# Rotary attention and two expert layers on one core: the opening cut into pieces, and pair 1's rotations dealt out between row maxima

## The chip, the cores and the metric

One of the eight cores of a Trainium2 chip runs the whole program. The metric is the device time of one execution in microseconds (us), lower is better.

## The reference, cut to what matters

```python
# q, k, v: 4 batches x 8 heads x 576 positions x 64, float32
q_rot, k_rot = rotate(q), rotate(k)        # x1*cos - x2*sin, x1*sin + x2*cos
scores = q_rot @ k_rot^T / 8
attn = exp(scores - rowmax(scores)); attn /= rowsum(attn) + 1e-9
x = attn @ v                               # -> 2304 tokens x 512
# layer 1: the best of 8 experts for each token, relu(x @ w1[e]) @ w2[e] * gate
# layer 2: relu(x @ w_in)^2 @ w_out        # 2304 x 512 -> 2048 -> 512
```

## The kernel before, in words

**Stages.** Attention comes first, then routing and the experts, then the dense layer. Attention works on 16 pairs P of heads. The change touches only the first two pairs.

**A pair.** `load(P)` brings the tile `qk`: 128 partitions, the values and their swapped halves (w), keys and queries (n = 0, 1), 640 columns. `rotate` is three passes: multiply by the cosine, multiply by the sine, add. `high` copies the sum into a tile `XH` in the fast float format on ScalarE; `low` puts the remainder into `XL`. For pairs from 1 on `stack_up` copies pieces of both into the tiles kZ, qZ and QH by DMA; for pair 0 `direct_high` and `direct_low` write them with ScalarE and VectorE. Then come nine row tiles s = 0 to 8. For each of them there are three steps, written here as S(P,s), the products on TensorE (`scores`), M(P,s), the row maximum on VectorE (`smax`), and X(P,s), the exponential on ScalarE (`sexp`). The scores have two PSUM buffers, so a third S waits for the X two before it. `turn` transposes exponentials on TensorE, `turned` copies them out on VectorE or ScalarE, `values`, `project` and `finish` do the rest.

**Who rotates.** Pairs 0 and 1 are rotated on VectorE, in `prepare`. From pair 2 on GpSimd does it, in three steps (`rope`, lines 394 to 396), and `low` without an engine argument is on GpSimd as well, for pair 1 too.

**The order.** Each engine carries out its instructions in the order in which the program issues them. `prepare()` is issued first; everything after it is put on a list with a due time, `OFF[...] + 15.954 * P`, and issued in the order of these times. The due times only sort; they are not waited for. The ones that matter here, in that unit:

```python
rope of pair 2 (GpSimd)          20.629, 23.559, 26.489
S(1,2) (TensorE)                 31.625
high(2) (ScalarE)                32.143
S(1,8) (TensorE)                 33.025
X(1,2) (ScalarE)                 33.433
low(2) (GpSimd)                  33.583
S(1,4) (TensorE)                 34.689
```

So on ScalarE `high(2)` stands ahead of X(1,2), and on GpSimd `low(1)`, issued by `prepare`, stands ahead of the three rope steps of pair 2. `prepare` also puts 14 products of 512 columns on TensorE ahead of pair 0's scores (line 169), and `scores` of pair 0 begins with two products whose result is overwritten (line 266).

Of the kernel before, what the change touches and what calls it, by code (L numbers as in the profile page):

```python
# [10 lines left out]
F32 = mybir.dt.float32  # L11
# [48 lines left out]
def shape_constants():  # L60
# [27 lines left out]
    for b in range(B):  # L88
        for c in range(4):
# [21 lines left out]
           un=[32.589, 32.153, 35.217, 38.036, 36.617, 23.748, 28.906, 37.6, 35.653, 34.253, 33.817],  # L111
           out=[33.418, 34.148, 36.917, 39.025, 37.411, 29.788, 32.958, 38.405, 36.294, 35.538, 34.643],
           av=[41.194, 44.969], x=[46.747, 47.789], pj=54.426, fin=58.03)
ON_DVE = [(0, 0), (0, 3), "LQ", "CR", (1, 0), (1, 1), (1, 3)]


def attention(tc, rope, ident, qk, v, w_gate, xd, on_batch, later, ahead):
# [24 lines left out]
    def ppt(name, shape=(128, 512)):  # L142
        return psa.tile(list(shape), F32, name=name, tag="pp", bufs=4)

    def prepare():
        nc.scalar.dma_start(out=TB[:, :, 0], in_=rope)
        load(0)
        load(1)
        for t in Xs:
            nc.gpsimd.memset(t[:, 576:640], 0.0)  # L150
        for t in SS:
            nc.gpsimd.memset(t[:, :, 1:2], 1e-9)
        for two in QH:
            for j in range(2):
                nc.gpsimd.memset(two[j][64 - 64 * j:128 - 64 * j].bitcast(F32), 0.0)
        nc.gpsimd.memset(R, 0.0)
        for r in range(2):
            d = slice(64 * r, 64 * r + 64)
            nc.gpsimd.tensor_copy(R[d, :, r, 0:64], ident[d, d].unsqueeze(1).broadcast_to([64, 4, 64]))
        for o, lo, hi in ((0, 64, 640), (576, 0, 64)):  # L160
            nc.scalar.activation(TB[:, :, 1, o:o + hi - lo], TB[:, :, 0, lo:hi], AF.Copy, scale=0.125)
        for j in range(2):
            Z = T["qZ", j] = zp.tile([128, 640], F32R, name="qZ", tag="qZ", bufs=4)
            nc.gpsimd.memset(Z[64 - 64 * j:128 - 64 * j, 0:512].bitcast(F32), 0.0)
        rotate(0, 0, nc.vector)
        high(0, 0)
        w = ppt("warm")
        for i in range(14):
            nc.tensor.matmul(w, T["hi", 0][:, 0, 0:128], T["hi", 0][:, 0, 0:512], start=True, stop=True)
        rotate(0, 1, nc.vector)  # L170
        direct_high(0)
        low(0, 0, nc.vector)
        direct_low(0, nc.vector)
        load(2)
        rotate(1, None, nc.vector)
        high(1)
        low(1)
        load_v(0)
        stack_up(1)

    def direct_high(P):


        x, h = T["qk", P], T["hi", P]
        for j in range(2):
            r = slice(64 * j, 64 * j + 64)
            nc.scalar.activation(QH[P][j][r], x[r, 0, 1, 0:512], AF.Copy)
        nc.scalar.activation(h[:, 1, 512:640], x[:, 0, 1, 512:640], AF.Copy)

    def direct_low(P, eng):  # L190
        x = T["qk", P]
        for j in range(2):
            r = slice(64 * j, 64 * j + 64)
            minus(eng, T["qZ", 2 * P + j][r, 0:512], x[r, 0, 1, 0:512], QH[P][j][r].bitcast(F32))
        minus(eng, T["lo", P][:, 1, 512:640], x[:, 0, 1, 512:640], T["hi", P][:, 1, 512:640].bitcast(F32))

    def gate_weights():
        for r in range(2):
# [3 lines left out]
    def load(P):  # L202
        t = T["qk", P] = ldp.tile([128, 2, 2, 640], F32, name="qk", tag="qk", bufs=2)
        src = qk[P].rearrange("p (w n c) -> p w n c", w=2, n=2)
        if P == 0:
            for n in range(2):
                nc.sync.dma_start(out=t[:, :, n], in_=src[:, :, n])
        else:
            nc.sync.dma_start(out=t, in_=src)

# [1 line left out]
        V = T["V", P] = wp.tile([128, 2, 5, 64], F32, name="V", tag="V", bufs=2)  # L212
        nc.sync.dma_start(out=V, in_=v[P].rearrange("p (h c d) -> p h c d", h=2, c=5))

    def rotate(P, n, eng, step=None):
        x, a = T["qk", P], slice(0, 2) if n is None else slice(n, n + 1)
        for i, (f, o, y) in enumerate(((times, 0, TB[:, 0, a]), (times, 1, TB[:, 1, a]), (plus, 0, x[:, 1, a]))):
            if step in (None, i):
                f(eng, x[:, o, a], x[:, o, a], y)

    def high(P, n=None):

        if ("hi", P) not in T:
            T["hi", P] = zp.tile([128, 2, 640], F32R, name="XH", tag="XH", bufs=2)
        a = slice(0, 2) if n is None else slice(n, n + 1)
        nc.scalar.activation(T["hi", P][:, a], T["qk", P][:, 0, a], AF.Copy)

    def low(P, n=None, eng=None):
        if ("lo", P) not in T:
            T["lo", P] = zp.tile([128, 2, 640], F32R, name="XL", tag="XL", bufs=2)  # L230
        a = slice(0, 2) if n is None else slice(n, n + 1)
        args = T["lo", P][:, a], T["qk", P][:, 0, a], T["hi", P][:, a].bitcast(F32)
        if eng is None:
            nc.gpsimd.tensor_sub(*args)
        else:
            minus(eng, *args)

    def stack_up(P, n=None):

        h, l = T["hi", P].bitcast(F32), T["lo", P].bitcast(F32)  # L240
        for j in range(2):
            r = slice(64 * j, 64 * j + 64)
            q = nc.scalar if P == 0 and j == 1 else nc.sync
            if n != 1:
                Z = T["kZ", 2 * P + j] = zp.tile([128, 640], F32R, name="kZ", tag="kZ", bufs=4)
                for i in range(2):
                    q.dma_start(out=Z[64 * i:64 * i + 64].bitcast(F32), in_=h[r, 0])
            if n != 0:
                Z = T["qZ", 2 * P + j] = zp.tile([128, 640], F32R, name="qZ", tag="qZ", bufs=4)
                q.dma_start(out=Z[0:64].bitcast(F32), in_=h[r, 1])  # L250
                q.dma_start(out=QH[P % 2][j][r].bitcast(F32), in_=h[r, 1, 0:512])
                q.dma_start(out=Z[64:128].bitcast(F32), in_=l[r, 1])

    def scores(P, s):

        t = T["S", P, s] = ps.tile([128, 2, 512], F32, name="ps", tag="ps", bufs=2)
        if s < 8:
            j, c = divmod(s, 4)
            todo, qs, qh = [j], slice(c * 128, c * 128 + 128), QH[P % 2][j]
            qh = qh[:, qs]  # L260
        else:
            todo, qs, qh = [0, 1], slice(512, 640), T["hi", P][:, 1, 512:640]
        k0 = 0 if s in (4, 5, 6, 7) else 64
        if P == 0:
            for u in range(2):
                nc.tensor.matmul(t[:, u, 0:288], QH[0][0][:, 0:128], T["hi", 0][:, 0, 0:288], start=True, stop=True)
            H, L = T["hi", P], T["lo", P]
            ql = L[:, 1, 512:640] if s == 8 else T["qZ", 2 * P + j][:, qs]
            for i, (q1, k1) in enumerate(((qh, H), (ql, H), (qh, L))):
                for u in range(2):  # L270
                    nc.tensor.matmul(t[:, u, 0:288], q1, k1[:, 0, k0 + 288 * u:k0 + 288 * u + 288], start=i == 0, stop=i == 2)
            return
        for i, j in enumerate(todo):
            Q1, K1 = T["qZ", 2 * P + j], T["kZ", 2 * P + j]
            for u in range(2):
                nc.tensor.matmul(t[:, u, 0:288], Q1[:, qs], K1[:, k0 + 288 * u:k0 + 288 * u + 288], start=i == 0, stop=False)  # L276
        for u in range(2):
            nc.tensor.matmul(t[:, u, 0:288], qh, T["lo", P][:, 0, k0 + 288 * u:k0 + 288 * u + 288], start=False, stop=True)  # L278
# [103 lines left out]
            at(t, lambda: route(P, t))  # L382

    prepare()
    at(24.0, gate_weights)
    for P in range(NPAIR):
        def on(o, f, *args):
            at(OFF["pair"] * P + o, lambda: f(*args))

        if P > 2:  # L390
            on(OFF["load"], load, P)
        if P > 0:
            on(OFF["v"] + (1.8 if P == NPAIR - 1 else 0), load_v, P)
        if P > 1:
            for i in range(3):
                on(OFF["rope"] + 2.93 * i, rotate, P, None, nc.gpsimd, i)
            on(OFF["hi"], high, P)
            on(OFF["lo"], low, P)
            on(OFF["z"], stack_up, P)
        for s in range(9):  # L400
            on(OFF["S"][s], scores, P, s)
            on(OFF["max"][s], smax, P, s)
            on(OFF["exp"][s], sexp, P, s)
        for un, o, o2 in zip(UNITS, OFF["un"], OFF["out"]):
            on(o, turn, P, un)
            on(o2, turned, P, un)
        for u in range(2):
            on(OFF["av"][u], values, P, u)
            on(OFF["x"][u], gathered, P, u)
        on(OFF["pj"], project, P)  # L410
        on(OFF["fin"], finish, P)
        if P % 4 == 3 and P + 1 < NPAIR:
            on(OFF["fin"] + .02, route, P)
# [10 lines left out]
def minus(v, out, a, b):  # L424
    v.tensor_tensor(out=out, in0=a, in1=b, op=ALU.subtract)
# [836 lines left out]
```

## Time and profile before

| | |
|---|---|
| median of 3 runs | 981.23 us (980.25 to 981.56) |
| profiled execution: its own time, its span | 979.74 us, 977.8 us |
| TensorE busy over the span | 953.0 us (97%) |
| VectorE, ScalarE, GpSimd busy | 530.7, 421.4, 322.0 us |
| attention, from the start to the last `project` | about 297 us |

The page shares the span out in 40 slices of 24.4 us. TensorE is at 4 tenths in the first slice and at 9 in all others but the last, at 7. In the trace the nine X of pair 0 start at 19.84, 20.56, 22.87, 23.94, 25.92, 27.41, 28.96, 30.46 and 32.00 us; the one that starts at 33.90 is X(1,2). All times below are us from the start of the span. The timeline merges neighbours of one kind: "x2" is two instructions, and the duration is from the start of the first to the end of the last.

### The profile page before, as it was taken

How to read it: one execution, taken by the hardware profiler on the slowest of the kernel's cores; microseconds unless marked ns; L12 is line 12 of the kernel's file. 1: busy time of each engine (PE TensorE's matmuls, PEld its weight loads, DVE VectorE, ACT ScalarE, POOL GpSimd, SP SyncE). 2: the span in 40 equal slices, each digit the busy share in tenths (PEclk: the TensorE clock that was granted, in tenths of full speed). 3: DMA queues.
4: the chain of work that ended last, by engine and by line, in shares of the span. 5: the costliest groups of instructions: out<-in, count | busy, mean ns of one | idle time of the engine just before them, and what ended most of it. 6: DMA issues, size and time to landing. Idle time of an engine off the chain costs nothing. (4 is left out here: it accounts for less than half of the span.)

```text
span 977.8 us, 15396 instructions
## 1 busy us (share of the span) xinstructions
PE 953.0 (97%) x5519; PEld 817.1 (84%) x5519; DVE 530.7 (54%) x935; ACT 421.4 (43%) x834; POOL 322.0 (33%) x259
## 2 busy tenths in 40 slices
PE   4999999999999999999999999999999999999997
PEld 3787878788787888888888789999999999999996
DVE  5677877777867255683785479423323323223221
ACT  3666657575642233343464377422322322222221
POOL 4786887887485111241353300010000100100101
PEclk9999999999999999999999999999999999999999
DMA  6876777866642833364586433100100201000000
GB/s 229 247 198 193 233 210 189 254 179 165 184 130 89 306 107 127 116 206 153 186 284 219 145 99 120 33 33 1 44 22 1 65 1 33 33 1 1 33 1 33
DMA packets 45135, 119.81 MB, mean 123 GB/s; under 512 B 8176, under 2 KB 8176, under 8 KB 42608
## 3 DMA queue, kind: packets, MB, share of 16 engines
q1 hardware_dynamic: 39808, 101.58, 33.7%
q0 software_dynamic: 4960, 16.43, 4.9%
q8 instruction: 45, 0.74, 0.3%
q10 hardware_dynamic: 272, 0.66, 0.2%
q14 instruction: 50, 0.41, 0.1%
HBM read 79.93 MB, written 15.11 MB: 97 GB/s over the span
## 5 line engine op out<-in xcount | busy, mean ns | idle before, releaser
L1088 PE MATMUL o<-Wo,gs 128*128 128x512 f32 x864 | 215.0, 393 | 0.4 <-ACT gs L1077 0.4
L1067 PE MATMUL h<-xs,Wi 128*128 128x384 f32 x1008 | 189.6, 336 | 0.0
L1088 PEld LDWEIGHTS o<-Wo,gs 128*128 128x128 f32 x864 | 159.8, 188 | 29.3 <-ACT gs L1077 0.8
L1067 PEld LDWEIGHTS h<-xs,Wi 128*128 128x128 f32 x1008 | 178.2, 188 | 6.6
L1076 DVE SCALAR_TENSOR_TENSOR g<-h,r 128x384 f32<-128x384 f32 x80 | 44.6, 558 | 190.7 <-ACT r L1072 190.7
L293 ACT ACTIVATE e<-ps,mx 128x576 f32<-128x576 f32 x144 | 106.2, 740 | 83.1 <-DVE mx L286 82.9
L1103 POOL DMA_INDIRECT out_dram<-os,at x18 | 17.9, 992 | 369.9 <-DVE os L1098 310.7
L286 DVE TENSOR_REDUCE mx<-ps 128x1 f32<-128x576 f32 x144 | 105.9, 753 | 57.2 <-PE ps L278 50.4
L1072 ACT ACTIVATE r<-h 128x384 f32<-128x384 f32 x96 | 47.1, 490 | 204.7 <-PE h L1067 204.7
L890 PE MATMUL p_y<-W,hh 128*128 128x512 f32 x504 | 122.9, 399 | 0.8 <-ACTq L902 0.8
L861 PE MATMUL p_h<-W,xs 128*128 128x512 f32 x480 | 114.9, 394 | 0.0
L890 PEld LDWEIGHTS p_y<-W,hh 128*128 128x128 f32 x504 | 93.1, 188 | 22.2 <-ACTq L902 1.1
L861 PEld LDWEIGHTS p_h<-W,xs 128*128 128x128 f32 x480 | 88.5, 188 | 18.4 <-DVEq L902 0.7
L311 PE MATMUL pp<-ident,e 128*128 128x128 f32 x640 | 85.5, 273 | 1.3 <-DVE eT L327 1.0
L1078 DVE TENSOR_TENSOR gs<-g,gs 128x384 fp32r<-128x384 f32 x96 | 53.5, 558 | 56.0 <-ACT gs L1077 56.0
L433 POOL TENSOR_TENSOR qk<-qk,TB 128x1280 f32<-128x1280 f32 x28 | 81.4, 2923 | 0.0
L311 PEld LDWEIGHTS pp<-ident,e 128*128 128x128 f32 x640 | 74.5, 141 | 2.6 <-DVE eT L327 1.6
L1077 ACT ACTIVATE gs<-g 128x384 fp32r<-128x384 f32 x96 | 50.4, 525 | 50.5 <-DVE g L1076 50.0
L276 PE MATMUL ps<-kZ,qZ 128*128 128x288 f32 x300 | 71.5, 328 | 0.3
L338 PE MATMUL av<-eT,V 128*64 128x288 f32 x512 | 69.1, 412 | 0.0
L327 DVE COPY eT<-pp 128x512 f32<-128x512 f32 x96 | 64.3, 684 | 4.6 <-PE pp L311 2.7
L895 POOL DMA_INDIRECT yd<-yo,idx x21 | 21.2, 1012 | 126.5 <-DVE yo L894 94.6
(237 smaller groups left out, 1208.7 us busy)
## 6 DMA issues: line engine op xcount, KB each, us to landing
qk<-in_qk_dram SPq DMA_DIRECT2D x15, 1280.0 KB, 6.5
raw<-in_moe_w_dram SPq DMA_DIRECT2D x30, 512.0 KB, 5.1
kZ<-XH SPq DMA_DIRECT2D x60, 160.0 KB, 2.8
rawa<-in_moe_w_dram SPq DMA_DIRECT2D x18, 512.0 KB, 3.5
w<-in_moe_w_in_dram SPq DMA_DIRECT2D x8, 1024.0 KB, 5.4
w<-in_moe_w_out_dram SPq DMA_DIRECT2D x8, 1024.0 KB, 5.0
V<-in_v_dram SPq DMA_DIRECT2D x16, 320.0 KB, 2.9
qZ<-XH SPq DMA_DIRECT2D x30, 160.0 KB, 2.9
```

What stands on the lines that cost most here:

```text
L276: nc.tensor.matmul(t[:, u, 0:288], Q1[:, qs], K1[:, k0 + 288 * u:k0 + 288 * u + 288], start=i == 0, stop=False)
L286: nc.vector.tensor_reduce(small("mx", P, 9)[:, s:s + 1], T["S", P, s][:, :, 0:288], axis=AX.XY, op=ALU.max, negate=True)
L293: nc.scalar.activation(ed.rearrange("p (u n) -> p u n", u=2), T["S", P, s][:, :, 0:288], AF.Exp, bias=T["mx", P][:, s:s + 1], accum_out=SS ...
L311: nc.tensor.transpose(t[:, c * 128:c * 128 + 128], src, ident)
L327: nc.vector.tensor_copy(o, i)
L338: nc.tensor.matmul(t[64 * j:64 * j + 64], V[:, j, kc], eT[:, j, kc, cs] if kc < 4 else eL[:, cs], start=kc == 0, stop=kc == 4)
L433: v.tensor_tensor(out=out, in0=a, in1=b, op=ALU.mult)
L861: nc.tensor.matmul(t[u], s[:, a, k], W1[:, b, k, 512 * u:512 * u + 512], start=n == 0, stop=n == 11)
L890: nc.tensor.matmul(t, s[:, a, k], W2[:, b, k], start=n == 0, stop=n == 23)
L1067: nc.tensor.matmul(t, W[:, a, k, fs], s[:, c, k], start=n == 0, stop=n == 11)
L1078: nc.vector.tensor_sub(gs[:, 1], g, gs[:, 0].bitcast(F32))
L1088: nc.tensor.matmul(self.T["o", b][c], gs[:, a, 128 * c:128 * c + 128], W[:, w], start=(f == 0 and n == 0), stop=(f == 15 and n == 2))
```

## The change

`prepare` loads the rope tables and pair 0 in column pieces, rotates and splits them piece by piece (keys in two halves of 320, queries as A = 0 to 256 and Z = 256 to 640), and issues 30 products of the identity with itself in place of the 14 large ones. What followed in `prepare` moves into a list, `opening()`, whose due times 0.0, 0.1, ... put it before all else. Pair 1 is no longer rotated in one go of three passes over 1280 columns; it is six passes over 640 (keys, then queries), and they alternate on VectorE with pair 0's maxima. `high(1)`, `low(1)` and `stack_up(1)` follow in halves. The two idle products of pair 0's scores move behind the real ones. Four of pair 0's transposes (FIRST) get due times of 29.5 to 30.1 and come ahead of S(1,2). The due times of all other work stay.

```diff
+FIRST = [(0, 1), (0, 0), (1, 3), (1, 2)]
+    HALF, A, Z = (slice(0, 320), slice(320, 640)), slice(0, 256), slice(256, 640)
     def prepare():
-        nc.scalar.dma_start(out=TB[:, :, 0], in_=rope)
+        for h in HALF:
+            nc.scalar.dma_start(out=TB[:, :, 0, h], in_=rope[:, :, h])
...
-        for o, lo, hi in ((0, 64, 640), (576, 0, 64)):
+        for o, lo, hi in ((0, 64, 320), (256, 320, 640), (576, 0, 64)):
             nc.scalar.activation(TB[:, :, 1, o:o + hi - lo], TB[:, :, 0, lo:hi], AF.Copy, scale=0.125)
-        rotate(0, 0, nc.vector)
-        high(0, 0)
-        w = ppt("warm")
-        for i in range(14):
-            nc.tensor.matmul(w, T["hi", 0][:, 0, 0:128], T["hi", 0][:, 0, 0:512], start=True, stop=True)
-        rotate(0, 1, nc.vector)
-        direct_high(0)
+        T["warm"] = ppt("warm")
+        keep_warm(nc, ident, T["warm"][:, 0:128], 30)
+        for h in HALF:
+            rotate(0, 0, nc.vector, cols=h)
+            high(0, 0, h)
+        rotate(0, 1, nc.vector, cols=A)
+        direct_high(0, A)
         low(0, 0, nc.vector)
-        direct_low(0, nc.vector)
-        load(2)
-        rotate(1, None, nc.vector)
-        high(1)
-        low(1)
-        load_v(0)
-        stack_up(1)
+        direct_low(0, nc.vector, A)
+    def opening():
+        two = lambda s: (lambda: scores(0, s), lambda: smax(0, s), lambda: sexp(0, s))
+        S, M, X = [dict(zip(range(9), [two(s)[n] for s in range(9)])) for n in range(3)]
+        step = lambda n, i: lambda: rotate(1, n, nc.vector, i)
+        return [S[0], S[1], lambda: rotate(0, 1, nc.vector, cols=Z), lambda: direct_high(0, Z), M[0], X[0], M[1], X[1],
+                lambda: direct_low(0, nc.vector, Z), lambda: load(2), S[4], S[5], step(0, 0), M[4], X[4], step(0, 1), M[5], X[5],
+                step(0, 2), S[8], S[2], M[8], X[8], lambda: high(1, 0), lambda: stack_up(1, 0),
+                step(1, 0), M[2], X[2], step(1, 1), S[3], S[6], M[3], X[3], step(1, 2), lambda: high(1, 1), M[6], X[6],
+                lambda: low(1, 1), lambda: low(1, 0), lambda: stack_up(1, 1), lambda: load_v(0), S[7], M[7], X[7]]
...
     def load(P):
-        if P == 0:
-            for n in range(2):
-                nc.sync.dma_start(out=t[:, :, n], in_=src[:, :, n])
+        if P < 2:
+            for n, c in ([(0, h) for h in HALF] + [(1, A), (1, Z)] if P == 0 else [(n, slice(0, 640)) for n in range(2)]):
+                nc.sync.dma_start(out=t[:, :, n, c], in_=src[:, :, n, c])
...
     prepare()
+    for n, f in enumerate(opening()):
+        at(.1 * n, f)
...
-        for s in range(9):
+        for s in range(9) if P else ():
...
+            if P == 0 and un in FIRST:
+                o, o2 = [t + .2 * FIRST.index(un) for t in (29.5, 29.6)]
```

`keep_warm` is `for i in range(n): nc.tensor.matmul(out, ident, ident, start=True, stop=True)`, in float32. `stack_up` now issues, for each head of a pair, first the kZ copies (n != 1) and then qZ from XH, QH, and qZ from XL (n != 0), all on SP.

## Rows read from the trace of the kernel before

**Rows 1.** Stretches of attention: sum and mean of the five from 34.77 to 240.
```profile
sum 205.23, PE 205.03 PEld 168.20 DVE 154.12 ACT 136.05 POOL 161.40; mean PE 41.01 PEld 33.64 DVE 30.82 ACT 27.21 POOL 32.28
```
**Rows 2.** Timeline, pair 1 to pair 2: start, duration, engine, line, tile<-sources, count [idle before].
```profile
18.66 1.27 ACT L226 ACTIVATE XH<-qk 128x1280 fp32r<-128x1280 f32 x1 [5.14 <-DVE qk L429]
20.08 2.93 POOL L234 TENSOR_TENSOR XL<-qk,XH 128x1280 fp32r<-128x1280 f32 x1 [13.65 <-ACT XH L226]
22.96 5.80 POOL L433 TENSOR_TENSOR qk<-qk,TB 128x1280 f32<-128x1280 f32 x2
28.85 2.93 POOL L429 TENSOR_TENSOR qk<-qk 128x1280 f32<-128x1280 f32 x1
32.73 1.26 ACT L226 ACTIVATE XH<-qk 128x1280 fp32r<-128x1280 f32 x1
33.90 0.73 ACT L293 ACTIVATE e<-ps,mx 128x576 f32<-128x576 f32 x1
34.77 0.53 PE L276 MATMUL ps<-kZ,qZ 128*128 128x288 f32 x2
```
**Rows 3.** Timeline of VectorE in the opening.
```profile
7.12 1.56 DVE L433 TENSOR_TENSOR qk<-qk,TB 128x640 f32<-128x640 f32 x2 [6.13 <-DMA qk<-in_qk_dram]
9.46 1.55 DVE L433 TENSOR_TENSOR qk<-qk,TB 128x640 f32<-128x640 f32 x2
11.79 0.82 DVE L425 TENSOR_TENSOR XL<-qk,XH 128x640 fp32r<-128x640 f32 x1
12.57 1.41 DVE L425 TENSOR_TENSOR qZ<-qk,QH 64x512 fp32r<-64x512 f32 x2
14.22 2.89 DVE L433 TENSOR_TENSOR qk<-qk,TB 128x1280 f32<-128x1280 f32 x2
18.55 1.41 DVE L286 TENSOR_REDUCE mx<-ps 128x1 f32<-128x576 f32 x2
```
**Rows 4.** DMA of the first loads: KB each and us to landing.
```profile
TB<-in_rope_dram ACTq DMA_DIRECT2D x1, 640.0 KB, 4.6
qk<-in_qk_dram SPq DMA_DIRECT2D x1, 640.0 KB, 6.3
```
**Rows 5.** DMA queue from 5 to 6, then 9 to 10: packets, MB, share.
```profile
q1 hardware_dynamic: 155, 0.40, 102.2%
...
q1 hardware_dynamic: 40, 0.41, 97.0%
```
**Rows 6.** Timeline, when the identity stands ready on GpSimd.
```profile
1.16 0.28 POOL masks.py:199 TENSOR_SCALAR_AFFINE_SELECT ident<-ident 128x128 f32<-128x128 f32 x1
```
**Rows 7.** Timeline of TensorE: the 14 products, two of the scores, a `project`.
```profile
10.37 6.32 PE L169 MATMUL warm<-XH 128*128 128x512 f32 x14 [10.37 <-ACT XH L226]
...
16.79 0.42 PE L271 MATMUL ps<-XH,QH 128*128 128x288 f32 x2
...
54.13 1.39 PE L349 MATMUL pj<-R,X 128*128 128x144 f32 x10
```
**Rows 8.** Timeline, one turn of pair 0's ring of scores.
```profile
26.61 0.76 DVE L286 TENSOR_REDUCE mx<-ps 128x1 f32<-128x576 f32 x1 [0.73 <-PE ps L271]
...
27.41 0.74 ACT L293 ACTIVATE e<-ps,mx 128x576 f32<-128x576 f32 x1 [0.66 <-DVE mx L286]
...
28.29 0.54 PE L266 MATMUL ps<-XH,QH 128*128 128x288 f32 x2 [0.17 <-ACT e L293]
...
29.67 0.76 DVE L286 TENSOR_REDUCE mx<-ps 128x1 f32<-128x576 f32 x1 [0.75 <-PE ps L271]
```
**Rows 9.** The copies of `stack_up`: an issue on SP, and landing times of qZ.
```profile
26.11 0.60 SPq L252 DMA_DIRECT2D qZ<-XL  x1
...
DMA to landing us min/median/max: 2.6/2.9/3.2
```
**Rows 10.** The end of the span: TensorE's last products, and a stretch after them.
```profile
966.55 5.27 PE L1088 MATMUL o<-Wo,gs 128*128 128x512 f32 x21 [0.40 <-ACT gs L1077]
...
975.50:976.00 0.50, 0.00 (x0) 0.00 (x0) 0.00 (x0) 0.00 (x0) 0.00 (x0) 0.68 0.01 0
```

More of the change, by code (lines that the diff above doesn't have):

```diff
@@ L155, in prepare @@
                 nc.gpsimd.memset(two[j][64 - 64 * j:128 - 64 * j].bitcast(F32), 0.0)
+        for j in range(2):
+            q = T["qZ", j] = zp.tile([128, 640], F32R, name="qZ", tag="qZ", bufs=4)
+            nc.gpsimd.memset(q[64 - 64 * j:128 - 64 * j, 0:512].bitcast(F32), 0.0)
         nc.gpsimd.memset(R, 0.0)
@@ L159, in prepare @@
             nc.gpsimd.tensor_copy(R[d, :, r, 0:64], ident[d, d].unsqueeze(1).broadcast_to([64, 4, 64]))
-        for o, lo, hi in ((0, 64, 640), (576, 0, 64)):
+        for o, lo, hi in ((0, 64, 320), (256, 320, 640), (576, 0, 64)):
             nc.scalar.activation(TB[:, :, 1, o:o + hi - lo], TB[:, :, 0, lo:hi], AF.Copy, scale=0.125)
-        for j in range(2):
-            Z = T["qZ", j] = zp.tile([128, 640], F32R, name="qZ", tag="qZ", bufs=4)
-            nc.gpsimd.memset(Z[64 - 64 * j:128 - 64 * j, 0:512].bitcast(F32), 0.0)
@@ L165, in prepare @@
-        rotate(0, 0, nc.vector)
-        high(0, 0)
-        w = ppt("warm")
-        for i in range(14):
-            nc.tensor.matmul(w, T["hi", 0][:, 0, 0:128], T["hi", 0][:, 0, 0:512], start=True, stop=True)
-        rotate(0, 1, nc.vector)
-        direct_high(0)
-        low(0, 0, nc.vector)
-        direct_low(0, nc.vector)
-        load(2)
-        rotate(1, None, nc.vector)
-        high(1)
-        low(1)
-        load_v(0)
-        stack_up(1)
-    def direct_high(P):
+        T["warm"] = ppt("warm")
@@ new lines, in prepare, with warm @@
+        keep_warm(nc, ident, T["warm"][:, 0:128], 30)
[4 more added lines that the diff above has]
+        direct_high(0, A)
+        low(0, 0, nc.vector)
+        direct_low(0, nc.vector, A)
+    def warm(n):
+        nc.tensor.matmul(T["warm"][:, 0:n], T["hi", 0][:, 0, 0:128], T["hi", 0][:, 0, 0:n], start=True, stop=True)
+    def opening():
[7 more added lines that the diff above has]
+                lambda: low(1, 1), lambda: low(1, 0), lambda: stack_up(1, 1), lambda: load_v(0), S[7], M[7], X[7]]
@@ L184, in direct_high @@
+    def direct_high(P, cols):
         x, h = T["qk", P], T["hi", P]
+        to = min(cols.stop, 512)
         for j in range(2):
             r = slice(64 * j, 64 * j + 64)
-            nc.scalar.activation(QH[P][j][r], x[r, 0, 1, 0:512], AF.Copy)
-        nc.scalar.activation(h[:, 1, 512:640], x[:, 0, 1, 512:640], AF.Copy)
-    def direct_low(P, eng):
+            nc.scalar.activation(QH[P][j][r, cols.start:to], x[r, 0, 1, cols.start:to], AF.Copy)
+        if cols.stop > 512:
+            nc.scalar.activation(h[:, 1, 512:640], x[:, 0, 1, 512:640], AF.Copy)
@@ L191, in direct_low @@
+    def direct_low(P, eng, cols):
         x = T["qk", P]
+        to = min(cols.stop, 512)
         for j in range(2):
             r = slice(64 * j, 64 * j + 64)
-            minus(eng, T["qZ", 2 * P + j][r, 0:512], x[r, 0, 1, 0:512], QH[P][j][r].bitcast(F32))
-        minus(eng, T["lo", P][:, 1, 512:640], x[:, 0, 1, 512:640], T["hi", P][:, 1, 512:640].bitcast(F32))
+            minus(eng, T["qZ", 2 * P + j][r, cols.start:to], x[r, 0, 1, cols.start:to], QH[P][j][r, cols.start:to].bitcast(F32))
+        if cols.stop > 512:
+            minus(eng, T["lo", P][:, 1, 512:640], x[:, 0, 1, 512:640], T["hi", P][:, 1, 512:640].bitcast(F32))
@@ L213, in load_v, with rotate, high @@
         nc.sync.dma_start(out=V, in_=v[P].rearrange("p (h c d) -> p h c d", h=2, c=5))
-    def rotate(P, n, eng, step=None):
+    def rotate(P, n, eng, step=None, cols=slice(0, 640)):
         x, a = T["qk", P], slice(0, 2) if n is None else slice(n, n + 1)
-        for i, (f, o, y) in enumerate(((times, 0, TB[:, 0, a]), (times, 1, TB[:, 1, a]), (plus, 0, x[:, 1, a]))):
+        for i, (f, o, y) in enumerate(((times, 0, TB[:, 0, a, cols]), (times, 1, TB[:, 1, a, cols]), (plus, 0, x[:, 1, a, cols]))):
             if step in (None, i):
-                f(eng, x[:, o, a], x[:, o, a], y)
-    def high(P, n=None):
+                f(eng, x[:, o, a, cols], x[:, o, a, cols], y)
+    def high(P, n=None, cols=slice(0, 640)):
         if ("hi", P) not in T:
@@ L225, in high @@
         a = slice(0, 2) if n is None else slice(n, n + 1)
-        nc.scalar.activation(T["hi", P][:, a], T["qk", P][:, 0, a], AF.Copy)
+        nc.scalar.activation(T["hi", P][:, a, cols], T["qk", P][:, 0, a, cols], AF.Copy)
     def low(P, n=None, eng=None):
@@ L238, in stack_up @@
     def stack_up(P, n=None):
-        h, l = T["hi", P].bitcast(F32), T["lo", P].bitcast(F32)
+        h = T["hi", P].bitcast(F32)
         for j in range(2):
             r = slice(64 * j, 64 * j + 64)
-            q = nc.scalar if P == 0 and j == 1 else nc.sync
+            todo = []
             if n != 1:
-                Z = T["kZ", 2 * P + j] = zp.tile([128, 640], F32R, name="kZ", tag="kZ", bufs=4)
-                for i in range(2):
-                    q.dma_start(out=Z[64 * i:64 * i + 64].bitcast(F32), in_=h[r, 0])
+                k = T["kZ", 2 * P + j] = zp.tile([128, 640], F32R, name="kZ", tag="kZ", bufs=4)
+                todo += [(k[64 * i:64 * i + 64], h[r, 0]) for i in range(2)]
             if n != 0:
[L249 to L252, printed above, removed]
+                q = T["qZ", 2 * P + j] = zp.tile([128, 640], F32R, name="qZ", tag="qZ", bufs=4)
+                todo += [(q[0:64], h[r, 1]), (QH[P % 2][j][r], h[r, 1, 0:512]), (q[64:128], T["lo", P].bitcast(F32)[r, 1])]
+            for o, i in todo:
+                nc.sync.dma_start(out=o.bitcast(F32), in_=i)
     def scores(P, s):
@@ L264, in scores @@
         if P == 0:
-            for u in range(2):
-                nc.tensor.matmul(t[:, u, 0:288], QH[0][0][:, 0:128], T["hi", 0][:, 0, 0:288], start=True, stop=True)
             H, L = T["hi", P], T["lo", P]
@@ L271, in scores @@
                     nc.tensor.matmul(t[:, u, 0:288], q1, k1[:, 0, k0 + 288 * u:k0 + 288 * u + 288], start=i == 0, stop=i == 2)
+            for u in range(2):
+                warm(288)
             return
```

## The prediction, made before the changed kernel was run

> **What bounds the kernel now.** I read the page's busy slices first: TensorE is idle for more than half of the first 24 us slice and full from then on. The stretches of attention say the same more sharply: from 34.77 to 240 us TensorE is busy for 205.03 of 205.23 us, while VectorE has 154 and GpSimd 161 [rows 1]. So from 34.77 on attention is bound by TensorE. What shifts the product that starts at 34.77 shifts everything behind it, in either direction, and there is no idle time behind it that could give a loss back. That product is S(1,4). The question is when it starts in the changed kernel.
>
> Then I followed the timeline back from it [rows 2]. S(1,4) starts 0.87 after X(1,2) at 33.90, which frees its PSUM buffer. X(1,2) stands behind high(2) on ScalarE, which starts at 32.73. high(2) needs pair 2's rotation on GpSimd, which ends at 28.85 + 2.93 = 31.78: in time, by 0.95 us. That rotation, 22.96 to 31.78, stands behind low(1) on GpSimd (20.08 to 22.96), and low(1) waits for high(1) at 18.66, which starts as VectorE ends pair 1's rotation. This line from VectorE through GpSimd to ScalarE is hidden today by less than a microsecond, and the change makes its first link later.
>
> **Prices on VectorE** [rows 3]. Three passes over 640 columns take 7.12 to 9.46, so 0.78 each; three over 1280 take 14.22 to 18.55, so 1.44 each. That is 0.12 and about 1.03 ns per column: 0.45 for 320 columns, 0.38 for 256, 0.52 for 384. low of 640 columns is 0.78 (11.79 to 12.57). direct_low, two of 512 columns on half the partitions and one of 128, takes 12.57 to 14.22; I split it into 0.80 for A and 1.05 for Z, as estimates. A row maximum is 0.75 (two in 1.41).
>
> **First pieces.** The rope table, 640 KB, landed at 0.74 + 4.6 = 5.34, the first keys at 0.74 + 6.3 = 7.04 [rows 4]. Half of each is as many bytes as the whole table: 5.3 at best, and 6.2, halfway to 7.04, if both halves of the table go first. I take 5.8. The second half of the keys has as many bytes ahead of it as before: 7.04, or a little later, because rows get half as long. Packets of 10 KB moved 0.41 MB in a microsecond at 97%, those of 2.6 KB 0.40 at 102% [rows 5], 8% less; as much again over some 3.5 us of traffic is 0.3, so 7.35. The Trainium skill ("DMA: Bandwidth & Descriptors", Specifications) has line rate from 512 bytes up, thus no loss at all; the rows differ already above that, and by the rule the sum below would be 0.3 less.
>
> **Identity products.** The identity is ready at 1.44 [rows 6], so 30 products start near 1.5. Each is two records of TensorE, as in a `project`, where five products are ten records of 144 columns in 1.39 us [rows 7]: 0.22 to 0.25 for 128 columns, twice that at the low clock. The 14 products took 6.32 us, 0.45 for 512 columns, the 1.2 GHz level, and the two scores after them 0.42 for 288 each, the 2.4 GHz level: the clock rose after about 6 us of products. (The profile's granted clock says 1.00 there; it has no record so early.) If it is so again, 12 to 14 are done by 7.7 and the rest by 11.2 to 12.2. S(0,0) can start when VectorE has written qZ's A, at about 11.4: a delay of 0 to 0.4, and I take 0. Low to the end would be 30 x 0.5 = 15 us and hold the first maxima back by up to 5.
>
> **VectorE's new chain.** Keys, first half: 5.8 to 7.15. Second half from 7.35: to 8.7. Queries A, 3 x 0.38: 9.84. low 0.78: 10.62. direct_low A: 11.42. Queries Z, 3 x 0.52: 12.98. M(0,0) and M(0,1): 14.48. direct_low Z: 15.53. Then pair 1's six passes with five maxima between them, 6 x 0.78 + 5 x 0.75 = 8.43: **24.0**, against 18.6 before. VectorE does not starve in it: a turn of the ring takes 3.06 per two scores (26.61 to 29.67, [rows 8]), with two idle products of 0.27 in front that move behind, so 1.4 per score, and a maximum with a rotation pass takes 1.53. So pair 0's maxima are done at about 26 instead of 32: the gain that the change can have. But the last rotation pass of pair 1 is 5.4 later, although the first started 1.3 earlier: 12.2 us of pair 0's work and maxima stand before or between what was one block.
>
> **From there on.** M(0,3) starts at 22.4, X(0,3) 0.80 later, which holds ScalarE for 0.93, so high(1,1) runs from 24.2 to 24.9 (half of 1.27 and a start). GpSimd begins at 25.0. Two halves of low cost 2.93, to 27.95; the three rope steps of pair 2 behind them cost 8.82 as before: **36.8** instead of 31.78. ScalarE has finished pair 0 and its early copies by 29 and waits at high(2). Queued behind it are X(1,2), X(1,8) and all later exponentials, and TensorE waits for these. X(1,2) starts 1.17 after high(2): 38.0, and S(1,4) at **38.9** instead of 34.77. The cover of 0.95 is gone and 4.1 us stand on the path. The four early transposes are no gain: both kernels have done them before S(1,4). Bounds of this term: pieces at 5.3 and 7.04 and maxima at 0.70 make it 3.4; later identity products make it 4.5, the low clock throughout up to 9.
>
> S(1,2) and S(1,8) don't set it: the last copy for head 0 is issued after low(1,1) at 26.5 and lands 2.9 later [rows 9], and head 1's three issues later, at 31.2; S(1,8) ends at 32.0.
>
> **The clock.** TensorE then has nothing to do from 32.0 to 38.9. The rows show what a pause does: the last products end at 971.8, and between 975.5 and 976.0 the granted clock leaves 1.00 (mean 0.68, then 0.50) [rows 10], some 3.9 us after the last product. So the pause should end at the low level. How long it lasts then has its only row in the opening, about 6 us of products at half speed: a loss of 3.05 if TensorE is the bound for all of them, 0 if the clock holds. I take 2.4, nearer to the row, because the first scores of pair 1 also wait for their ring. The Trainium skill ("TensorE: Matmul & The Clock Gate", HAM oscillation) speaks against the change in the same way: a kernel whose products pause for their operands pays the slow start after every pause, at a price of half of the time spent at the half rate. With the 6 us of the row that is the 3.05; it gives no other result.
>
> **Sum.** 4.1 + 2.4 = 6.5 us slower. On the profiled execution 979.74 becomes 986.2; it lies 1.5 under the median of 981.23, so by the median **987.7**. The other parts cost nothing: extra issues on SP and ScalarE's queue stand before 6 us, under the loads that they start; warm-up products behind the scores run while TensorE waits for the ring; load(2) leaves SP at about 15.5 and has landed by 22, before GpSimd asks at 28.
>
> **Rivals.** (a) The same wait, but the clock holds, because S(1,2) and S(1,8) break the pause or the fall comes late: 4.1, 985.3. For it: one row of a fall, at the end of the program. Against: 6.9 us is well over 3.9.
> (b) Faster: high(2) finds its operand in time, and TensorE runs through to S(1,4) right behind S(1,8), at 32.0, 2.8 earlier: 978.4. For it: pair 0's maxima do end 6 us sooner. It decides where GpSimd can begin low(1,1) by 21, that is 11.75 before 32.73, so VectorE's last rotation pass by 20; I get 24.0, and only at an average of 0.4 per step, which no row has, would it be there. GpSimd at a higher speed while VectorE is idle would do it too, but low(1) took 2.93 at 20.08, with VectorE idle for most of it, and the others 2.9 beside a busy one [rows 2].
> (c) In between: GpSimd begins two to three microseconds sooner than by my sum, and the wait shrinks to within 2 us of before: 981 to 983.
> (d) The change doesn't do what it says: identity products don't raise the clock, and hold TensorE to 16: 5 more, 992.7. Against: the 14 did raise it.
>
> **How the numbers follow.** Forecast 0.60, (a) 0.22, (b) 0.07, (c) 0.06, (d) 0.05. The likeliest alone gives 986 to 989. From (a) at its lower bound, 3.4 less 1 for the run, to the clock's full 3.05 with late identity products and 2 for the unknown rest: 983.6 to 991.0; outside lie (b), (d) and part of (c). A measurement of this kernel can tell 0.2% (2 us) from no change. Faster 0.07, same 0.05, slower 0.88.
>
> **What would show it.** In the changed kernel's timeline: pair 1's last addition on VectorE ends near 24, GpSimd's rope steps of pair 2 run from 28 to 37, ScalarE idles from 29 to 37 with high(2) waiting on GpSimd, X(1,2) comes near 38, and TensorE has a pause of 5 us or more before S(1,4), with products twice as long after it. The prediction is wrong if high(2) starts before 33, if GpSimd's rope steps begin before 24, or if TensorE waits again later so that the shift is not carried to the end.

## The result, and the profile after

The changed kernel takes 986.11 us (median of 4 executions, 984.3 to 987.75) against 981.03 (median of 4, 980.25 to 981.56): 1.0052 times as long, interval 1.0039 to 1.0065, so 5.1 us slower. Its profiled execution was the fastest of the four, 984.3, with a span of 982.5 instead of 977.8.

The page of the changed kernel shows the loss and not its place: TensorE is busier in the first slice, at 8 instead of 4, and has a dent in the second, and so has its granted clock, which was at 9 in every slice before.

```profile
span 982.5 us, 15516 instructions
...
PE   8699999999999999999999999999999999999997
...
PEclk9799999999999999999999999999999999999999
```

The timeline of the changed kernel gives the place. These lines answer to [rows 2], in the same order: high(1) in its second half, low(1), pair 2's rotation on GpSimd, high(2), X(1,2), S(1,4).

```profile
23.18 0.74 ACT L243 ACTIVATE XH<-qk 128x640 fp32r<-128x640 f32 x1
...
24.06 3.05 POOL L251 TENSOR_TENSOR XL<-qk,XH 128x640 fp32r<-128x640 f32 x2 [17.27 <-ACT XH L243]
...
27.07 5.75 POOL L453 TENSOR_TENSOR qk<-qk,TB 128x1280 f32<-128x1280 f32 x2
...
32.89 2.88 POOL L449 TENSOR_TENSOR qk<-qk 128x1280 f32<-128x1280 f32 x1
35.80 1.27 ACT L243 ACTIVATE XH<-qk 128x1280 fp32r<-128x1280 f32 x1 [7.92 <-POOL qk L449]
36.98 0.72 ACT L309 ACTIVATE e<-ps,mx 128x576 f32<-128x576 f32 x1
...
37.85 0.85 PE L292 MATMUL ps<-kZ,qZ 128*128 128x288 f32 x2 [6.38 <-ACT e L309]
```

The brackets tell it: ScalarE stood idle for 7.92 us in front of high(2), released by GpSimd's addition, and TensorE for 6.38 us in front of S(1,4), released by the exponential behind high(2). S(1,4) starts 3.08 later than before. Then the scores run at half speed: two products of 288 columns take 0.85 where they took 0.53. The stretches of the changed kernel around it (length; busy time of TensorE, its weight loads, VectorE, ScalarE, GpSimd, each with a count; granted clock, where 1.00 is TensorE's full speed and 0.50 half of it; DMA share, GB/s):

```profile
31.00:37.00 6.00, 0.46 (x2) 0.12 (x1) 0.76 (x1) 1.20 (x2) 4.69 (x2) 0.50 0.82 311
37.00:40.50 3.50, 2.65 (x12) 2.64 (x13) 0.76 (x1) 2.01 (x6) 3.35 (x2) 0.50 0.59 134
40.50:41.00 0.50, 0.50 (x5) 0.50 (x4) 0.08 (x1) 0.50 (x3) 0.50 (x1) 0.73 0.91 197
```

From there on nothing is given back. The first and the last of the 16 `project` of the changed kernel, against 54.13 [rows 7] and 296.10 before, are 4.30 and 4.25 later; the fourteen between are 4.25 to 4.31 later. Before the change (one line), then after it (two):

```profile
296.10 1.49 PE L349 MATMUL pj<-R,X 128*128 128x144 f32 x10 [0.99 <-ACT X L341]
...
58.43 1.39 PE L365 MATMUL pj<-R,X 128*128 128x144 f32 x10
...
300.35 1.49 PE L365 MATMUL pj<-R,X 128*128 128x144 f32 x10 [0.99 <-ACT X L357]
```

So of the 4.3, 3.1 are the wait; the other 1.2 I put down to the low clock, which e4 below confirms. And the opening did become faster. VectorE's lines answer to [rows 3]: the first pass starts at 5.44 instead of 7.12 and the first row maximum at 12.88 instead of 18.55, but pair 1's rotation, which ended at 18.6, starts at 15.32 and ends with the addition at 22.33.

```profile
5.44 1.09 DVE L453 TENSOR_TENSOR qk<-qk,TB 128x320 f32<-128x320 f32 x2 [4.44 <-DMA TB<-in_rope_dram]
...
12.88 1.41 DVE L302 TENSOR_REDUCE mx<-ps 128x1 f32<-128x576 f32 x2
...
15.32 0.82 DVE L453 TENSOR_TENSOR qk<-qk,TB 128x640 f32<-128x640 f32 x1
...
21.66 0.75 DVE L302 TENSOR_REDUCE mx<-ps 128x1 f32<-128x576 f32 x1
22.33 0.81 DVE L449 TENSOR_TENSOR qk<-qk 128x640 f32<-128x640 f32 x1
23.06 0.75 DVE L302 TENSOR_REDUCE mx<-ps 128x1 f32<-128x576 f32 x1
```

### The profile page after: what moved, and what is told of

The parts are those of the page before. It is cut to its first block, busy times and chain, and to the rows that moved or that the text cites. A ratio compares the mean times of both kernels' runs of the same rounds, so it can differ in the third digit from the quotient of the medians.

```text
span 982.5 us, 15516 instructions
## 1 busy us (share of the span) xinstructions
PE 958.4 (98%) x5565; PEld 823.2 (84%) x5565; DVE 532.6 (54%) x946; ACT 422.2 (43%) x839; POOL 322.7 (33%) x260
## 5 line engine op out<-in xcount | busy, mean ns | idle before, releaser
L292 PEld LDWEIGHTS ps<-kZ,qZ 128*128 128x128 f32 x300 | 45.5, 191 | 23.9 <-ACT e L309 8.9
```

## The experiments

Each was timed beside the kernel before on its chip; ratios are to that, with intervals. Theory G: the loss is high(2) waiting for GpSimd, which is late because pair 1's rotation ends late. Rival P: the pieces, the identity products or the order of the copies cost the time. Rival C: the low clock is most of it. Edits are shortened where "..." stands.

**e1_block: only the dealing out undone.**

```diff
-  ..., S[4], S[5], step(0,0), M[4], X[4], step(0,1), M[5], X[5], step(0,2), ..., step(1,2), high(1,1), ...
+  ..., S[4], S[5], step(0,0), step(0,1), step(0,2), step(1,0), step(1,1), step(1,2), high(1,0), high(1,1),
+  low(1,1), low(1,0), stack_up(1,0), stack_up(1,1), load_v(0), M[4], X[4], M[5], X[5], S[8], ...
```

> Of the change, only the dealing out of pair 1's rotation is undone: its six passes stand in one block ahead of M(0,4); pieces, identity products and early transposes stay. Theory G (the loss is high(2) waiting for GpSimd's rotation of pair 2, which starts late because pair 1's rotation ends late): VectorE ends pair 1's rotation near 20 instead of 23.1, GpSimd ends pair 2's near 32.7, X(1,2) near 33.9, S(1,4) near 34.8 as before, no long pause of TensorE: 981, 5 less than the changed kernel. Rival P (the pieces, the identity products or the new order of the copies cost the time): 985 to 986, as these stay.

Measured: 981.34, ratio 1.0016 (1.0007 to 1.0026). The pieces, the identity products and the early transposes are all in it, and some 3.5 of the 5 us are gone. Rival P falls: at most the rest, 1.6 us by the ratio, is left for it. GpSimd, ScalarE and TensorE lines of e1:

```profile
30.63 2.92 POOL L449 TENSOR_TENSOR qk<-qk 128x1280 f32<-128x1280 f32 x1
...
33.58 1.27 ACT L243 ACTIVATE XH<-qk 128x1280 fp32r<-128x1280 f32 x1 [0.74 <-POOL qk L449]
...
35.62 0.85 PE L292 MATMUL ps<-kZ,qZ 128*128 128x288 f32 x2 [2.09 <-ACT e L309]
...
56.42 1.39 PE L365 MATMUL pj<-R,X 128*128 128x144 f32 x10
```

high(2) waits for 0.74 instead of 7.92. S(1,4) is still 0.85 later than before the change, and it starts at the low clock; the first `project` is 2.29 later. This execution took 983.78, 2.4 more than the median of the eleven (980.52 to 985.29); TensorE's last product ends 4.1 later than in the kernel before, 1.9 of that behind attention, which the change does not touch. What is left in an execution near the median was not traced.

**e2_low_on_vector: GpSimd's link cut.**

```diff
-  ..., lambda: low(1, 1), lambda: low(1, 0), ...
+  ..., lambda: low(1, 1, nc.vector), lambda: low(1, 0, nc.vector), ...
```

> The changed kernel with low(1) on VectorE instead of GpSimd: the dealing out stays, the link through GpSimd is cut. Theory G: GpSimd's rotation of pair 2 starts when its load lands, near 21.7, and ends near 30.5 instead of 35.7; X(1,2) near 31.7, S(1,4) near 32.6, that is 2.2 earlier than before the change: 978.8. Rival P: 985 or more, with VectorE loaded by another 1.6.

Measured: 983.41, ratio 1.0028 (1.0015 to 1.0041). A miss of 4.6, and an instructive one. GpSimd began pair 2's rotation at 22.89 as meant, while VectorE still had a rotation pass and both low to do:

```profile
22.01 0.82 DVE L453 TENSOR_TENSOR qk<-qk,TB 128x640 f32<-128x640 f32 x1
22.75 0.75 DVE L302 TENSOR_REDUCE mx<-ps 128x1 f32<-128x576 f32 x1
23.41 3.10 DVE L449 TENSOR_TENSOR qk<-qk 128x640 f32<-128x640 f32 x1
26.44 0.75 DVE L302 TENSOR_REDUCE mx<-ps 128x1 f32<-128x576 f32 x1
27.32 6.04 DVE L445 TENSOR_TENSOR XL<-qk,XH 128x640 fp32r<-128x640 f32 x2
```

Passes with two inputs from SBUF take 3.0 to 3.1 us instead of 0.8 when GpSimd is at work on one of its own; maxima, which read PSUM, stay at 0.75. GpSimd's three steps become 6.38 (two) and 3.34 for 5.80 and 2.93. The Trainium skill ("SBUF — State Buffer", Who interferes with whom) has the rule: a VectorE instruction with two SBUF inputs contends with a GpSimd instruction that reads SBUF, because its second input comes through a read interface that the two share. The trace agrees: each VectorE pass takes about as long as one GpSimd pass (2.9). I had priced low on VectorE at 1.6. e2's loss is about half of the changed kernel's (2.8 thousandths for 5.2), but its eight executions spread from 981.15 to 986.59, and the traced one took 985.99. In it high(2) no longer waits for GpSimd; M(0,7) behind the two low is what is late (33.29), and S(1,4) starts at 39.33. So e2 tells the rivals apart only weakly.

**e3_before_pool_busy: the same wait made in the kernel before.**

```diff
+    def busy():
+        o = wp.tile([128, 512], F32, name="busy", tag="busy", bufs=1)
+        for i in range(4):
+            times(nc.gpsimd, o, TB[:, 0, 0, 0:512], TB[:, 0, 1, 0:512])
+    at(20.0, busy)
```

> The kernel before the change with four extra GpSimd products of 512 columns (about 1.2 each, 4.7 in all; their result is not used) between low(1) and the rotation of pair 2, nothing else. Theory G: the 0.95 of cover goes and 3.8 are on the path: high(2) near 36.5, S(1,4) near 38.5, and with a low clock after the pause 1 to 3 more: 985 to 987.5. Rival P: nothing of the opening's pieces is in it, so it stays at 981.

Measured: 985.96, ratio 1.0058 (1.0044 to 1.0072). Nothing of the change is in it, and the loss is like it, 5.5 us by the medians, for a wait that is 1.1 longer. GpSimd's 5.3 us of extra work stand in front of pair 2's rotation; 0.95 were covered, and S(1,4) is 4.21 later:

```profile
22.82 5.34 POOL L438 TENSOR_TENSOR busy<-TB 128x512 f32<-128x512 f32 x4
...
36.94 1.27 ACT L226 ACTIVATE XH<-qk 128x1280 fp32r<-128x1280 f32 x1 [3.47 <-POOL qk L434]
...
38.98 0.81 PE L276 MATMUL ps<-kZ,qZ 128*128 128x288 f32 x2 [3.53 <-ACT e L293]
```

**e4_filled_pause: the clock's part.**

```diff
+    def busy(n):
+        if "busy" not in T:
+            T["busy"] = ppt("busy")
+        keep_warm(nc, ident, T["busy"][:, 0:128], n)
+    for t, n in ((31.6, 5), (33.0, 5), (33.1, 24)):
+        at(t, lambda n=n: busy(n))
```

> The changed kernel with 34 more identity products on TensorE (0.22 each at the high clock; result not used) in its pause, 5 ahead of S(1,2), 5 ahead of S(1,8), 24 behind it, so that the clock finds no pause. Theory G with the low clock as a second, smaller term: high(2) and S(1,4) stay near 35.8 and 37.9, but the products behind it run at the high clock: 1.2 to 3 less than the changed kernel, 983 to 985. Rival C (the low clock is most of the loss): back to 981 to 982. If the clock is not concerned: 986 as it is.

Measured: 983.28, ratio 1.0035 (1.0021 to 1.0048). high(2) starts at 35.87 and S(1,4) at 37.91, as in the changed kernel, but at full speed. S(1,4) is 3.14 late and so is the first `project`, instead of 4.30: with the clock up, nothing is lost behind the wait. The granted clock stays at 1.00:

```profile
31.00:37.00 6.00, 5.53 (x50) 5.33 (x48) 0.76 (x1) 1.13 (x1) 4.76 (x2) 1.00 0.85 315
...
37.91 0.52 PE L292 MATMUL ps<-kZ,qZ 128*128 128x288 f32 x2 [1.38 <-ACT e L309]
```

In the two traces the clock's part is thus 1.2 of 4.3. By the medians the loss goes from 5.1 to 2.9 us, so 2.2 would be the clock's; by the ratios it is 1.7, and their intervals overlap, so the times alone do not settle it. The clock is a real second term, the wait the first; rival C falls. Five executions of this kernel lie within 1.6 us; the changed one has two near 984.5 and two near 987.6. That the low stretch has a different length in each would explain it, but only one of them was traced.

**e5_one_identity.**

```diff
-        keep_warm(nc, ident, T["warm"][:, 0:128], 30)
+        keep_warm(nc, ident, T["warm"][:, 0:128], 1)
```

> The changed kernel with 1 identity product instead of 30. Theory G: pair 0's scores then start at the low clock, 8 products of 288 columns take 2.1 instead of 1.07, the first maxima come later, and as each rotation pass of pair 1 stands behind a maximum, its end, GpSimd's rotation and S(1,4) move with them: S(1,4) 1 to 3 later than 37.85, 987 to 989. If the identity products do nothing for the path: 986 as it is.

Measured: 985.92, ratio 1.0054 (1.0041 to 1.0068): like the changed kernel, and below the 987 to 989 that theory G gave. The mechanism shows in small: without the products the first scores take 0.82 for two instead of 0.51, and S(1,4) comes at 38.74, 0.89 later. The time doesn't show it. The products that warm the clock are worth under a microsecond at S(1,4).

**e6_high_after_x4, e7_high_after_x0, e8_before_high_later: high behind the exponentials, in every pair.**

```diff
-OFF = dict(pair=15.954, load=-26.0, v=8.0, rope=-11.279, hi=0.235, lo=1.675, z=4.815,
+OFF = dict(pair=15.954, load=-26.0, v=8.0, rope=-11.279, hi=4.435, lo=4.575, z=4.815,    # e6
+OFF = dict(pair=15.954, load=-26.0, v=8.0, rope=-8.879, hi=6.8, lo=6.9, z=6.95,          # e7, and e8 on the kernel before
```

> The changed kernel, with only the due times of high and low moved from 0.235 and 1.675 to 4.435 and 4.575 in every pair, so that high(2) stands behind X(1,2), X(1,8) and X(1,4) on ScalarE instead of ahead of them. GpSimd is as late as before. Theory G: S(1,4) no longer waits and comes near 31.5, behind S(1,8); the wait for GpSimd (rotation of pair 2 ends at 35.8) moves to X(1,1), near 37.1 against 38.08 before the change: about 1 faster than before, 979.5, if no low clock adds to it. Rival P (pieces and copies cost the time, not the wait at high(2)): 985 or more.

> The changed kernel with high, low, the copies and the rotation steps of GpSimd put later in every pair (due 6.8, 6.9, 6.95 and -8.879), so that high(2) stands behind X(1,0) as well. Theory G: GpSimd is ready at 35.8 when ScalarE comes to it, TensorE runs on from S(1,8) at 30.3, and most of the gain of the earlier opening appears: S(1,4) near 31.2, 2 to 3.5 faster than before: 977 to 979; S(2,2) or S(2,8) can wait up to 1.5 for the later copies. Rival P: 985 or more.

> The kernel before the change with the same later due times as e7_high_after_x0, as its control. Theory G: high(2) did not wait there (0.95 of cover), so its place is worth nothing: within 1 of 980.4; a gain here would mean that e7's comes from the order alone and not from the opening.

Measured: 996.75 (1.0170, 1.0153 to 1.0187), 1089.8 (1.1116, 1.1101 to 1.1131) and 1097.45 (1.1186, 1.1171 to 1.1201). All three expectations missed. The first 40 us of e7 are as theory G has it, and then it loses. S(1,4), the first product of the values, and the queue behind them in e7:

```profile
31.68 0.42 PE L292 MATMUL ps<-kZ,qZ 128*128 128x288 f32 x2
...
37.75 2.16 PE L354 MATMUL av<-eT,V 128*64 128x288 f32 x16
...
41.17 0.33 SPq L226 DMA_DIRECT2D qk<-in_qk_dram  x1
...
41.55 1.15 SPq L268 DMA_DIRECT2D kZ<-XH  x2
...
52.30 0.82 PE L292 MATMUL ps<-kZ,qZ 128*128 128x288 f32 x2 [7.97 <-DMA qZ<-XL]
```

S(1,4) starts at 31.68 in e7 and at 30.90 in e6, against 34.77 before and 37.85 in the changed kernel. The first product of the values starts at 37.75, before the change at 40.51: with high(2) out of the way the earlier opening is worth 2.8 us at this point. The order alone is not: e8, the kernel before with the same order, has it at 41.08. The kernel before, then e8:

```profile
40.51 2.16 PE L338 MATMUL av<-eT,V 128*64 128x288 f32 x16
...
41.08 2.16 PE L338 MATMUL av<-eT,V 128*64 128x288 f32 x16
```

But the copies' new due time, 6.95, put them behind load(4) (5.91) on SP's queue. That load waits for GpSimd's low(2) to free its buffer, so pair 2's copies start at 41.55 though XH was ready at 38.1, and S(2,2) waits 7.97 for them. The next twelve pairs lose another 7 to 9 each, and the granted clock falls in each of these waits; the control e8 waits 7.86 at the same place. I had moved a DMA past another one without pricing the queue. e6, in which no copy moved, was 2.6 late at its first `project`, lost 0.25 more in most of the next pairs, about 1.6 in two, and 8.0 and 2.2 in two late ones; why was not pursued.

**e9_high_late_pairs_2_to_5 and e10_high_late_pairs_2_to_4: only while GpSimd is late.**

```diff
+# due after the pair's base, by pair; others as they were          e9                              e10
+HI = {2: 6.75, 3: 4.4, 4: 3.0, 5: 1.6}                                        # {2: 4.435, 3: 3.0, 4: 1.6}
+LO = {2: 6.76, 3: 4.6, 4: 3.2, 5: 1.8}                                        # {2: 4.575, 3: 3.2, 4: 1.8}
+ZS, ROPE, LOAD = {2: 6.78}, {3: 2.2}, {4: 1.0}   # ROPE, LOAD are added        # {2: 4.815}, {}, {}
+            for n in (0, 1) if P == 2 else (None,):
+                on(ZS.get(P, OFF["z"]), stack_up, P, n)
```

> The changed kernel with high and low later only while GpSimd catches up: high(2) behind X(1,0), high(3) behind X(2,4), high(4) behind X(3,8), high(5) behind X(4,2), all others in their old places; load(4) and the rotation of pair 3 stay behind low(2) and pair 2's copies, and those go out kZ first. Theory G: the first product of the values comes near 37.8 as in e7_high_after_x0, against 40.5 before the change and 44.8 in the changed kernel; S(2,2) or S(2,8) wait 1 to 2 for pair 2's copies, whose low is still 4 later than before the change; so 0.5 to 2 faster than before the change: 978.5 to 980. If the copies' wait grows past 3 us or the clock falls in it, slower than before: 981 to 984. Rival P: 985 or more.

> The smaller form: high(2) behind X(1,4), high(3) behind X(2,8), high(4) behind X(3,2), nothing else moved. Theory G: S(1,4) free, X(1,1) waits for GpSimd until about 37.1; the first product of the values about 41.1 as in e6_high_after_x4 (with a low clock after the wait in it), and nothing lost behind: 981 to 982, that is 4 to 5 less than the changed kernel. Rival P: 985 or more.

Measured: e9 980.77, ratio 1.0004 (0.9995 to 1.0013), no different from before the change, where I had expected 978.5 to 980; e10 984.17, 1.0035 (1.0024 to 1.0046), 2.2 above what I expected. In e9 the order in the queues alone (ScalarE's, GpSimd's and SP's) takes the whole 5 us off the changed kernel, with all of its pieces, identity products and early transposes in place. That settles where the 5 us stood. S(1,4) starts at 31.99 in e9 and at 31.49 in e10. e9 doesn't beat the kernel before, and its trace says why:

```profile
38.07 2.16 PE L355 MATMUL av<-eT,V 128*64 128x288 f32 x16
...
45.82 0.50 PE L293 MATMUL ps<-kZ,qZ 128*128 128x288 f32 x2 [1.16 <-DMA qZ<-XL]
...
53.27 1.49 PE L366 MATMUL pj<-R,X 128*128 128x144 f32 x10
```

It is 2.4 ahead at the first product of the values, 0.86 ahead at the first `project`, and 0.3 and 0.8 behind at the next two (70.83 and 87.81 against 70.56 and 86.99); there it stays. S(2,2) waits for the copy of what GpSimd's low(2) made, and S(3,s) for a high that came late. GpSimd ends pair 2's rotation at 37.00, 5.2 us later than in the kernel before, and high's place only decides which pair pays for that. Of the 5.2, 4.0 are the changed kernel's; the other 1.2 belong to this execution, in which pair 0's scores ran at a granted clock of 0.50 from 16 to 19 (1.00 in the trace of the changed kernel): X(0,1) ahead of that was 0.2 later than in the changed kernel, X(0,5) behind it 1.1.

## Why the prediction was right

The sign, the place and the mechanism held, step by step; the sizes were too large. The 986.11 lies 1.6 below the forecast and 0.8 above the 985.3 of rival (a), so the time does not tell these two apart. The trace does: S(1,4) took 0.85 instead of 0.53, at a granted clock of 0.50. Rival (a), the wait without the low clock, is what e4 made: 983.28, with a wait of 3.1 and not 4.1.

- **TensorE bounds from S(1,4) on, and a shift is carried to the end.** Held: 4.30 at the first `project`, 4.25 at the last.
- **First pieces at 5.8 and 7.35.** 5.44 and 7.25. The row length cost at most 0.2.
- **Identity products cost nothing.** They ended at 10.9, as qZ's first piece was written, and M(0,0) came at 12.88 (predicted 12.98).
- **VectorE's chain to 24.0.** It ended at 23.14. This is the term that was mis-sized: I gave a pass and a maximum 1.53 together, and they take 1.40 (maxima at 21.66 and 23.06): VectorE starts the next instruction before the last one's recorded end (the addition is recorded to 23.14, the maximum behind it from 23.06). Six passes and five maxima took 7.8 instead of 8.4. (The 12.2 us of other work that the prediction counts there are 13.3 by its own terms; its sum does not use them.)
- **GpSimd to 36.8.** 35.77: it began 0.9 sooner and its steps were 8.7 instead of 8.82.
- **The wait is 4.1.** 3.08, just under my lower bound of 3.4, by the two points above. e3 makes a delay of 4.2 at the same place and loses 5.5.
- **The pause, and the clock falling in it, 2.4.** The pause was 6.4 (6.9 predicted). The clock fell, but already near 30.5, in the loose stretch around S(1,2) and S(1,8), and rose near 40.8, so only 2.9 us of work ran at half speed: 1.2 in the traced execution, 2.2 by the medians of the changed kernel and e4. Forecast 6.5 in all, the terms came to 4.3 in the trace. The price was in the range, the moment of the fall not.
- **Rival (b).** It asked for GpSimd to begin by 21; it began at 24.06. Its gain, 2.8, is what e7 shows at the first product of the values when high(2) is out of the way.
- **Rivals (c) and (d).** (c) asked for GpSimd to begin two to three us sooner than by my sum; it was 0.9, and the wait stayed over 2. (d) asked for identity products that leave the clock low; the first scores took 0.51 for two, and 0.82 in e5, without them.

## What to carry to other kernels

An opening that feeds a chain over three engines does not become faster because its first stage hands out its first results sooner; it does when the operand of the last link is there sooner. Look for the instruction that waits at the head of an in-order queue (here a copy for the pair after next), take the slack of the engine that feeds it from the trace, and compare it with what the change adds in front. When such an order is mended, move it for the pairs that need it, and price every DMA that is moved past a waiting one.

## What the runs showed of the hardware that I had not expected

VectorE passes over 640 columns with both inputs in SBUF took 3.10 us, and two others 6.04 together, instead of 0.82 each beside GpSimd passes (e2), while GpSimd's own went from 5.80 for two and 2.93 to 6.38 and 3.34.

And the granted clock fell without a full pause: in the changed kernel at 30.5, after some 3 us in which TensorE had only S(1,2) and a part of S(1,8) to do. It does not follow from the program alone: in e6 TensorE did the same there (S(1,2) at 28.35, the second part of S(1,8) at 30.30), and the clock stayed at 1.00 until 38. Nor was it the same in the opening: from 16 to 19 it was 0.50 in the traces of e2, e7 and e9 and 1.00 in those of the changed kernel, e4, e6 and e10, whose instructions up to there are the same. In e1 it was low twice, from 22 to 25 after a pause of 4.31 and from 36 to 38.5 after a pause of 2.09; the second took 1.4 us (S(1,4) 0.85 late, the first `project` 2.29).
